# A gated mix of a Fourier layer and a token MLP on one core: operands of 512 columns in pairs of K tiles, PSUM banks in pairs

## The chip, the core and the metric

The kernel runs on one core of one Trainium2 chip. The metric is the device time of one execution in microseconds. Before the change its median over three runs is 1861.19 us (1860.97 to 1861.49).

A core has a matrix engine (TensorE, "PE" in the profile), whose weight loads are listed apart as "PEld", a vector engine (VectorE, "DVE"), a scalar engine (ScalarE, "ACT"), GpSimd ("POOL"), which here only issues DMAs, and SyncE ("SP"), which issues the loads. Each engine works through its own instructions in the order in which the program lists them and waits at an instruction until what it needs is there. SBUF is the on-chip memory that operands lie in, PSUM the one that matmuls write; PSUM has 8 banks of 512 float32 values per partition here.

## What is computed

```python
def _A_ref(x, dft_seq_re, dft_seq_im, dft_hid_re, dft_hid_im):
    a = jnp.einsum("bsd,ed->bse", x, dft_hid_re)
    b = jnp.einsum("bsd,ed->bse", x, dft_hid_im)
    return jnp.einsum("ts,bse->bte", dft_seq_re, a) - jnp.einsum("ts,bse->bte", dft_seq_im, b)

def _B_ref(x, w1, b1, w2, b2):
    h = _layernorm(x, axis=-1)
    u = _gelu(jnp.einsum("bsd,sf->bdf", h, w1) + b1)
    y = jnp.einsum("bdf,fs->bds", u, w2) + b2
    return y.transpose(0, 2, 1)

x = A_x
g = _sigmoid((x * gate_w).sum(-1, keepdims=True))
return g * _A_ref(x, ...) + (1 - g) * _B_ref(x, ...)
```

x is 2048 x 1024, the Fourier matrices are 2048 x 2048 and 1024 x 1024, w1 is 2048 x 3584 and w2 is 3584 x 2048, all float32.

## The kernel before

**Four stages.** Each large product is a stage, an object of a class derived from `Bilinear`: `Fourier` (q: x against the sequence matrices), `Mixed` (y: q against the hidden matrices), `Up` (u: w1 against the normalised x) and `Down` (o: w2 against u). They run one after another.

**26 products in place of 32.** A stage splits one operand into 4 x 4 blocks and the other into 4 x 2, and computes the 4 x 2 result with 26 block products instead of 32. The table `SCHEME` (line 48) lists for each product the signed sum of blocks of one operand, that of the other, and the signed result blocks to which it is added. The sums are formed on DVE (`add`, `sub`, lines 478 and 481), or by an accumulating DMA of POOL (`add_onto`, line 489); sums that return later are stored to DRAM (line 494). In the profile W names the operand that TensorE holds as weights, R the one that it streams.

**Three matmuls for one.** Each operand is split into a high half, rounded on ACT (line 508), and a low half, the difference, on DVE (lines 513 and 515). Lines 771 to 773 multiply high by high, high by low and low by high, each 128 x 128 weights against 128 x 512. A block holds `nk` K tiles of 128 rows: 4 in q, y and u, 7 in o. It gives `nm` x `nn` PSUM banks: 8 in q, 4 in y and o, 7 in u. `groups()` says in which steps the K tiles run; the last two always run together, bank by bank. One bank gets 3 matmuls a K tile. A product has 96 matmuls in q, 48 in y, 84 in u and o.

**Evictions and chains.** When a bank has its last K tile, each result block that reads it takes it over: first with a copy (`plain_copy`, on ACT or DVE), then with a multiply-add of one bank on DVE (`fused`, line 816). Where the signs of two products that follow each other agree well enough, the second goes on adding in the same banks (`self.chained`), and what it must not pass on is corrected by coefficients. PE then returns to a bank of which the eviction must be over. `self.reads` lists the blocks that read product j: one for most, two for some, three for one of u. In o every eviction is scaled by the gate, a scalar per partition (`hgate`, `ngate`).

**Order and memory.** Nothing of the order is written by hand. `Graph` collects tasks with a key (its due time in K steps) and `schedule()` plays them through with fixed costs; what is ready with the lowest key goes first. The order found is the program order of each engine. SBUF is two pools: 40 slots of 1024 columns ("f") and 23 of 512 ("h"); PSUM has 8 slots of one bank. Raw operands of 512 columns lie in h; the high and low halves of such an operand share one f slot in y and o (`pairs`) and lie in two h slots elsewhere. Result blocks lie in f slots, two banks to a slot.

In q only W has 512 columns, and R has 1024; in u only R has 512, and W has 896; in y and o both have 512.

Of the kernel before, what the change touches and what calls it, by code (L numbers as in the profile page):

```python
# [24 lines left out]
SLOTS = {"f": 40, "h": 23, "ps": 8}  # L25
# [3 lines left out]
HOP = 0.1  # L29
DMA_RATE = 330e3  # L30
# [240 lines left out]

class Task:
# [138 lines left out]
def gated_mix_kernel(  # L411
# [31 lines left out]
        "ps": (ctx.enter_context(tc.tile_pool(name="psum", bufs=8, space=bass.MemoryType.PSUM)), H),  # L443
# [138 lines left out]
    class Bilinear:  # L582
# [6 lines left out]
        pairs = False  # L589
        ahead = 3  # L590

        def __init__(self, name, nk, nm, nn, wn, rn, big, keep, order, extra, perm):
            self.name, self.nk, self.nm, self.nn = name, nk, nm, nn
            self.n = {"W": wn, "R": rn}
            self.big, self.perm = big, perm
            rows = [SCHEME[j] for j in order]

            self.small = "RW"[big == "R"]
            small = [r[1] for r in rows]
            self.again = {j: s for j in range(1, len(rows)) for s in (1, -1) if small[j] == [s * c for c in small[j - 1]]}  # L600
            self.kept = {}
            self.plan = {x: plan([None if x != big and j in self.again else r[x != big] for j, r in enumerate(rows)],
                                 extra[x != big], keep[x]) for x in "WR"}
            self.out = [r[2] for r in rows]
            self.val, self.saved, self.stored = {"W": {}, "R": {}}, {}, {}
            for x in "WR":
                for e in sorted(self.plan[x][1]):
                    for k in range(nk):
                        self.saved[x, e, k] = scratch(self.n[x], f"{name}_{x}{e}_{k}", 1)
            self.C, self.PS, self.half = {}, {}, {}  # L610
# [47 lines left out]
        def term(self, x, e, last, j, k, key):  # L658

            val, n = self.val[x], 16 if x == self.big else 8  # L660
            if (e, k) not in val:
                if e < n:
                    pi, pk, pj = self.perm
                    b = pi[e // 4] * 4 + pk[e % 4] if x == self.big else pk[e // 2] * 2 + pj[e % 2]
                    val[e, k] = self.block(x, b, j, k, key), 1
                else:
                    d, v = self.saved[x, e, k], slot(self.n[x], f"{self.name}_{x}{e}_p{j}_{k}")
                    load(key, v, d.t, (d,))
                    val[e, k] = v, self.stored[x, e, k]
            v, s = val.pop((e, k)) if last else val[e, k]  # L670
            return v, s, last and not (e < n and x in self.resident)

        def by_dma(self, x, j, k, o):
            return False

        def fresh(self, x, e, k, last):

            if (e, k) in self.val[x] or not last:
                return None
            if e < (16 if x == self.big else 8):  # L680
                pi, pk, pj = self.perm
                b = pi[e // 4] * 4 + pk[e % 4] if x == self.big else pk[e // 2] * 2 + pj[e % 2]
                return None if x in self.resident else (*self.source(x, b, k), 1)
            d = self.saved[x, e, k]
            return d.t, (d,), self.stored[x, e, k]

        def operand(self, x, j, k, key):
# [3 lines left out]
            for o, ((a, ca, la), (b, cb, lb)) in ops:  # L691
                if self.by_dma(x, j, k, o):
                    swap = self.fresh(x, a, k, la) is None
                    if swap:
                        (a, ca, la), (b, cb, lb) = (b, cb, lb), (a, ca, la)
                    src = self.fresh(x, a, k, la)
                    if src is not None and lb and fresh.get(b) != k and (b >= (16 if x == self.big else 8) or x not in self.resident):
                        held = (b, k) in self.val[x] or b < (16 if x == self.big else 8)
                        sb = self.val[x][b, k][1] if (b, k) in self.val[x] else self.stored.get((x, b, k), 1)
                        if held and ca * src[2] == cb * sb:  # L700
                            v, sb, _ = self.term(x, b, lb, j, k, key)
                            add_onto(key, v, *src[:2])
                            self.val[x][o, k] = v, cb * sb
                            if o in self.plan[x][1]:
                                d = self.saved[x, o, k]
                                self.stored[x, o, k] = cb * sb
                                fresh[o] = k
                                store(key + 1, d.t, d, v)
                            continue
                (va, sa, mine_a), (vb, sb, mine_b) = self.term(x, a, la, j, k, key), self.term(x, b, lb, j, k, key)  # L710

                mine_a, mine_b = mine_a and fresh.get(a) != k, mine_b and fresh.get(b) != k
                v = va if mine_a else vb if mine_b else slot(self.n[x], f"{self.name}_{x}s{o}_{k}")
                (add if ca * sa == cb * sb else sub)(key, v, va, vb)
                self.val[x][o, k] = v, ca * sa
                if o in self.plan[x][1]:
                    d = self.saved[x, o, k]
                    self.stored[x, o, k] = ca * sa
                    fresh[o] = k
                    store(key + 1, d.t, d, v)  # L720
            v, sv, _ = self.term(x, e, last, j, k, key)
            return v, s * sv

        def build(self):
            nonlocal step
            eps = 1
            for j in range(len(self.out)):
                self.during(j, step)
                for ks in self.groups():
                    ops = []  # L730
                    for k in ks:
                        pair, val = {}, {}
                        for x in "RW":
                            if x == self.small and j in self.again:
                                pair[x], s = self.kept[k]
                                val[x] = None, s * self.again[j]
                            else:
                                val[x] = self.operand(x, j, k, step)
                        s = val["R"][1] * val["W"][1]
                        if k == 0 and not self.chained[j]:  # L740
                            eps = s * self.sign[j]
                        flip = s != eps * self.sign[j]
                        for x in "RW":
                            if x not in pair:
                                v, s = val[x]
                                negate = flip and (x == "W" or self.small in pair)
                                pair[x] = self.split(x, step, v, j, k, negate)
                                if x == self.small:
                                    self.kept[k] = pair[x], -s if negate else s
                            elif x == self.small:  # L750
                                self.kept[k] = pair[x], val[x][1]
                        ops.append((pair["R"], pair["W"]))
# [3 lines left out]
        def split(self, x, key, v, j, k, negate):  # L756
            return split(key, v, f"{self.name}_p{j}_{x.lower()}_{k}", negate, self.pairs)

        def matmuls(self, j, ks, ops, eps):
            first, end = ks[0] == 0 and not self.chained[j], ks[-1] == self.nk - 1  # L760
            for m in range(self.nm):
                c = slice(m * P, (m + 1) * P)
                for n in range(self.nn):
                    if first:
                        self.PS[m, n] = View(Buf("ps", f"ps_{self.name}_p{j}_{m}_{n}"), 0, H)
                    bank, e = self.PS[m, n], slice(n * H, n * H + H)
# [425 lines left out]
```

## Time and profile before

| | us |
|---|---|
| median of the runs | 1861.19 |
| the profiled execution, its own time | 1859.57 |
| its span, first to last instruction | 1857.8 |
| TensorE busy (8122 matmuls) | 1848.7 |
| VectorE busy | 1687.8 |
| ScalarE busy | 893.7 |
| GpSimd busy | 249.7 |

The profile lists every instruction with its start and duration, which engine or DMA ended the idle time before it, and the DMA transfers. Its tables are read in four ways below: by stretches of time, with the busy time of each engine and (after "x") the instructions in the stretch; in order of time for one engine; by groups of like instructions; and along the chain of waits that ended last. The durations of matmuls overlap, since they are pipelined: the time that one costs is the distance of the starts. The same holds to a lesser degree for DVE and ACT.

### The profile page before, as it was taken

The page shows a single profiled execution, that of the slowest core. Times are in us where ns is not written, and L with a number is a line of the kernel's source. Part 1 is how long each engine was busy: PE and PEld are TensorE (multiplying, and loading weights), DVE is VectorE, ACT ScalarE, POOL GpSimd, SP SyncE. Part 2 cuts the span into 40 slices and gives each one's busy share as a digit, 9 for nine tenths or more (in the row PEclk, how much of TensorE's full clock was granted, in tenths as well). Part 3 has the DMA queues.
Part 4 walks back from the last instruction along what each step waited for, and adds up shares of the span by engine and source line. Part 5 has one row for each costly group of instructions (what it writes and reads, how often), then busy time and mean ns, then how long its engine had stood idle before and what let it go on. Part 6 is the DMA issues. An engine that isn't in the chain of part 4 may idle for free.

```text
span 1857.8 us, 24437 instructions
## 1 busy us (share of the span) xinstructions
PE 1848.7 (100%) x8122; PEld 1522.2 (82%) x8122; DVE 1687.8 (91%) x2443; ACT 893.7 (48%) x1379; POOL 249.7 (13%) x428
## 2 busy tenths in 40 slices
PE   9999999999999999999999999999999999999999
PEld 7888888888888888888888888888888888888787
DVE  8899679979979999999978699889799999998996
ACT  5443335644535555586554325345464535443442
POOL 1100010111022101112121211121120000001111
PEclk9999999999999999999999999999999999999999
DMA  9967478969698767989658798897988566675974
GB/s 381 332 229 257 166 241 317 332 250 392 225 317 306 215 229 241 329 287 342 223 191 293 254 356 318 285 369 252 357 310 285 164 204 205 213 230 120 273 199 99
DMA packets 199358, 491.88 MB, mean 265 GB/s; under 512 B 24832, under 2 KB 24832, under 8 KB 199232
## 3 DMA queue, kind: packets, MB, share of 16 engines
q1 hardware_dynamic: 159984, 369.72, 58.2%
q0 software_dynamic: 39104, 120.35, 19.7%
q8 instruction: 63, 1.03, 0.2%
q14 instruction: 63, 0.52, 0.1%
q10 hardware_dynamic: 144, 0.26, 0.0%
HBM read 375.41 MB, written 114.82 MB: 264 GB/s over the span
## 4 chain that ended last, share of the span: by engine, by line
PE 79%; DVE 11%; issue 5%; DMA 4%; POOL 1%; ACT 0%; SPq 0%; POOLq 0%; DVEq 0%; ACTq 0%
PE ps_q_p L773 10%; PE ps_q_p L772 10%; PE ps_q_p L771 10%; PE ps_u_p L773 9%; PE ps_u_p L772 9%; PE ps_u_p L771 9%; PE ps_o_p L771 5%; PE ps_o_p L772 5%; PE ps_o_p L773 5%; PE ps_y_p L771 3%; PE ps_y_p L773 3%; PE ps_y_p L772 3%; DVE o_W_p L478 1%; DVE y_c L816 1%; DVE o_p_r L515 1%
## 5 line engine op out<-in xcount | busy, mean ns | idle before, releaser
L771 PE MATMUL ps_q_p<-q_p_r_hi,q_p_w_hi 128*128 128x512 f32 x824 | 320.7, 389 | 1.1 <-ACT q_p_w_hi L508 1.1
L773 PE MATMUL ps_q_p<-q_p_r_hi,q_p_w_lo 128*128 128x512 f32 x824 | 320.6, 389 | 0.1
L772 PE MATMUL ps_q_p<-q_p_r_lo,q_p_w_hi 128*128 128x512 f32 x824 | 320.7, 389 | 0.0
L771 PE MATMUL ps_o_p<-o_p_r,o_p_w 128*128 128x512 f32 x728 | 284.5, 391 | 1.9 <-DVE o_c L816 1.6
L772 PE MATMUL ps_o_p<-o_p_r,o_p_w 128*128 128x512 f32 x728 | 283.3, 389 | 0.0
L773 PE MATMUL ps_o_p<-o_p_r,o_p_w 128*128 128x512 f32 x728 | 283.3, 389 | 0.0
L771 PE MATMUL ps_u_p<-u_p_r_hi,u_p_w_hi 128*128 128x512 f32 x728 | 283.2, 389 | 0.0
L773 PE MATMUL ps_u_p<-u_p_r_hi,u_p_w_lo 128*128 128x512 f32 x728 | 283.2, 389 | 0.0
L772 PE MATMUL ps_u_p<-u_p_r_lo,u_p_w_hi 128*128 128x512 f32 x728 | 283.2, 389 | 0.0
L771 PEld LDWEIGHTS ps_q_p<-q_p_r_hi,q_p_w_hi 128*128 128x128 f32 x824 | 154.7, 188 | 33.7 <-ACT q_p_w_hi L508 1.5
L773 PEld LDWEIGHTS ps_q_p<-q_p_r_hi,q_p_w_lo 128*128 128x128 f32 x824 | 154.7, 188 | 32.5 <-DVE q_p_w_lo L513 0.4
L772 PEld LDWEIGHTS ps_q_p<-q_p_r_lo,q_p_w_hi 128*128 128x128 f32 x824 | 154.7, 188 | 32.3 <-DVE q_p_r_lo L515 0.3
L508 ACT ACTIVATE o_p_r<-o_R_p 128x512 fp32r<-128x512 f32 x175 | 107.5, 626 | 134.2 <-DVE o_R_p L481 43.3
L508 ACT ACTIVATE q_p_r_hi<-q_R_p 128x1024 fp32r<-128x1024 f32 (+1 forms) x101 | 105.1, 1047 | 125.7 <-DVE q_R_p L478 70.3
L771 PEld LDWEIGHTS ps_o_p<-o_p_r,o_p_w 128*128 128x128 f32 x728 | 136.6, 188 | 34.5 <-DVE o_c L816 6.5
L508 ACT ACTIVATE o_p_w<-o_W_p 128x512 fp32r<-128x512 f32 x182 | 111.3, 626 | 110.1 <-DVE o_W_p L481 47.3
L508 ACT ACTIVATE u_p_w_hi<-u_W_p 128x896 fp32r<-128x896 f32 x104 | 97.8, 950 | 136.8 <-DVE u_W_p L478 91.2
L771 PE MATMUL ps_y_p<-y_p_r,y_p_w 128*128 128x512 f32 x416 | 162.5, 391 | 0.7 <-DVE y_c L816 0.5
L772 PE MATMUL ps_y_p<-y_p_r,y_p_w 128*128 128x512 f32 x416 | 161.9, 389 | 0.0
L773 PE MATMUL ps_y_p<-y_p_r,y_p_w 128*128 128x512 f32 x416 | 161.8, 389 | 0.0
L771 PEld LDWEIGHTS ps_u_p<-u_p_r_hi,u_p_w_hi 128*128 128x128 f32 x728 | 136.6, 188 | 28.6 <-DVE u_c L816 0.2
L773 PEld LDWEIGHTS ps_o_p<-o_p_r,o_p_w 128*128 128x128 f32 x728 | 136.6, 188 | 28.5
(150 smaller groups left out, 3283.4 us busy)
## 6 DMA issues: line engine op xcount, KB each, us to landing
q_R_p<-in_ct_dram SPq DMA_DIRECT2D x131, 512.0 KB, 6.9
u_W_p<-in_w_dram SPq DMA_DIRECT2D x136, 448.0 KB, 6.1
o_W_p<-in_w_dram SPq DMA_DIRECT2D x196, 256.0 KB, 5.2
o_R_p<-u SPq DMA_DIRECT2D x140, 256.0 KB, 4.6
u<-u_c POOLq DMA_DIRECT2D x126, 256.0 KB, 5.7
y_W_p<-q SPq DMA_DIRECT2D x99, 256.0 KB, 5.2
q<-q_c POOLq DMA_DIRECT2D x80, 256.0 KB, 6.0
q_W_p<-in_x_dram SPq DMA_DIRECT2D x75, 256.0 KB, 7.1
```

The costliest lines, as they stand in the source:

```text
L478: g.add({"DVE": dve(o.n)}, key, lambda e: nc.vector.tensor_add(o.ap, a.ap, b.ap), r=(a.reg, b.reg), w=(o.reg,))
L508: g.add({"ACT": act(v.n)}, key, lambda e: nc.scalar.activation(hi.ap, v.ap, AF.Copy, scale=-1.0 if negate else 1.0), r=(v.reg,), w=(hi.reg,))
L515: nc.vector.tensor_sub(lo.ap, v.ap, hi.ap.bitcast(F32))
L771: nc.tensor.matmul(bank.ap, wh.ap[:, c], rh.ap[:, e], start=a, stop=False, skip_group_check=True)
L772: nc.tensor.matmul(bank.ap, wh.ap[:, c], rl.ap[:, e], start=False, stop=False, skip_group_check=True)
L773: nc.tensor.matmul(bank.ap, wl.ap[:, c], rh.ap[:, e], start=False, stop=b, skip_group_check=True)
L816: lambda e: nc.vector.scalar_tensor_tensor(o.ap, ps.ap, scale, o.ap, op0=ALU.mult, op1=ALU.add),
```

## The change

An operand of 512 columns is handled for two K tiles at once. `unit` maps each K tile to its pair; `new` takes one f slot for both halves; raw blocks, sums, stored sums and the high and low halves are all of 1024 columns. Only the last K tile of o stays single. Operands of 1024 and 896 columns stay as they are.

PSUM has 4 slots of two banks. Two banks that follow each other are evicted by one instruction (`evacuate`), n before m; in u the seventh is alone. The key of an eviction is half a step lower (`EVAC`). In y and o the first two K tiles run together too (`groups`).

In o, blocks that end before the last product are accumulated without the gate and scaled by it in one ACT instruction a tile when they are done; the block that ends last is gated as before, bank by bank. The sums of w2 that an accumulating DMA made are all on DVE (`by_dma` no longer holds for any). Rows of h are normalised in halves. The pools are 49 f and 5 h slots. The start of the first product is written out as before, with W in two halves.

```diff
-SLOTS = {"f": 40, "h": 23, "ps": 8}
+SLOTS = {"f": 49, "h": 5, "ps": 4}
+EVAC = 0.5
...
+            self.unit = {x: [(k,) if n > H or nk - k == nk % 2 else (k - k % 2, k - k % 2 + 1) for k in range(nk)]
+                         for x, n in self.n.items()}
...
         def groups(self):
-            return [(k,) for k in range(self.nk - 2)] + [(self.nk - 2, self.nk - 1)]
+            return ([(0, 1)] if self.nm * self.nn == 4 else [(0,), (1,)]) + [(k,) for k in range(2, self.nk - 2)] + [(self.nk - 2, self.nk - 1)]
...
+        def new(self, x, name, u, parts=1):
+            n = self.n[x] * len(u)
+            return View(Buf("f" if n > H else "h", f"{self.name}_{x}{name}_{u[0]}", None, parts), 0, n)
+
-        def block(self, x, b, j, k, key):
-            src, r = self.source(x, b, k)
-            v = slot(self.n[x], f"{self.name}_{x}{b}_p{j}_{k}")
-            load(key, v, src, r)
+        def block(self, x, b, j, u, key):
+            v = self.new(x, f"{b}_p{j}", u, len(u))
+            for i, k in enumerate(u):
+                load(key, v.at(i, self.n[x]), *self.source(x, b, k))
             return v
...
+                if end and (i % 2 or i == count - 1):
+                    self.evacuate(j, i // 2, step + len(ks) + i / count - EVAC, i % 2 + 1, eps)
...
+        def new_bank(self, j, i):
+            b = self.PS[i - 1].buf if i % 2 else Buf("ps", f"ps_{self.name}_p{j}_{i}", None, 2)
+            self.PS[i] = View(b, i % 2 * H, H, i % 2)
+
+        def evacuate(self, j, i, key, count, eps):
+            bank = View(self.PS[2 * i].buf, 0, count * H, None if count == 2 else 0)
+            mn = [divmod(2 * i + t, self.nm)[::-1] for t in range(count)]
+            for q, coef in self.reads[j]:
+                b = self.perm[0][q // 2] * 2 + self.perm[2][q % 2]
+                o = self.C.get((b, i))
+                if o is None:
+                    o = self.C[b, i] = View(Buf("fh"[count == 1], f"{self.name}_c{b}_{i}", None, count), 0, count * H)
...
+                        self.copy(key, b, mn, o, bank, eps * coef)
+                else:
+                    self.accumulate(key, b, mn, o, bank, eps * coef)
+                if j in self.ends[b]:
+                    del self.C[b, i]
+                    for t, (m, n) in enumerate(mn):
+                        self.finish(key + 1, b, m, n, o.at(t, H), j)
...
     class Down(Bilinear):
...
-        def by_dma(self, x_, j, k, o):
-            return j > 1 and (k + j) % 7 in O_DMA
+        def by_dma(self, x_, j, u, o):
+            return j > 1 and (u[0] // 2 + j) % 4 in O_DMA
...
-        def accumulate(self, key, b, m, n, o, ps, coef):
-            i, t = (b // 2) * 4 + m, hgate if coef > 0 else ngate
-            fused(key, o, ps, t.t[:, i:i + 1], (t,))
+        def accumulate(self, key, b, mn, o, ps, coef):
+            if self.ends[b][0] < len(self.out) - 1:
+                return fused(key, o, ps, float(coef))
+            for t, (m, _) in enumerate(mn):
+                i, f = (b // 2) * 4 + m, hgate if coef > 0 else ngate
+                fused(key, o.at(t, H), ps.at(t, H), f.t[:, i:i + 1], (f,))
...
             if j == len(self.out) - 1:
                 store(key, dst, reg, o, "SP")
             else:
+                g.add({"ACT": act(H) + 0.15}, key, lambda e: nc.scalar.activation(
+                    o.ap, o.ap, AF.Copy, scale=hgate.t[:, i:i + 1]), r=(o.reg, hgate), w=(o.reg,))
                 g.add({"POOL": 0.9}, key, lambda e: nc.gpsimd.dma_start(dst, o.ap, accum_op=ALU.add),
                       r=(o.reg,), w=(reg,), nbytes=2.2 * P * o.n * 4)
```

More of the change, by code (lines that the diff above doesn't have):

```diff
@@ L731, in build @@
                     for k in ks:
-                        pair, val = {}, {}
                         for x in "RW":
[L734 to L739, printed above, removed]
+                            u = self.unit[x][k]
@@ L795, in c_slots @@
[L795 to L803 removed]
+            first, end, count = ks[0] == 0 and not self.chained[j], ks[-1] == self.nk - 1, self.nm * self.nn
```

275 lines of the change are left out of this document (123 added, 152 removed).

## The prediction

> **What bounds the kernel now.** I read the page's first lines first, then a table of stretches, one for each stage, with the busy time of every engine, then the list of who waited for whom on PE.
>
> ```profile
> span 1857.8 us, 24437 instructions
> PE 1848.7 (100%) x8122; PEld 1522.2 (82%) x8122; DVE 1687.8 (91%) x2443; ACT 893.7 (48%) x1379; POOL 249.7 (13%) x428
> ...
> core 0: us, PE busy (x) PEld busy (x) DVE busy (x) ACT busy (x) POOL busy (x), PEclk, DMA share, GB/s
> 5.55:573.50 567.95, 566.72 (x2496) 468.50 (x2497) 506.69 (x657) 267.60 (x401) 70.90 (x127) 1.00 0.81 289
> 573.50:858.70 285.20, 284.55 (x1250) 233.69 (x1249) 279.86 (x456) 169.07 (x271) 43.52 (x74) 1.00 0.81 267
> 858.70:1353.80 495.10, 495.10 (x2186) 409.84 (x2185) 432.61 (x573) 236.06 (x335) 87.14 (x163) 1.00 0.82 293
> 1353.80:1854.10 500.30, 498.36 (x2185) 408.86 (x2183) 467.03 (x758) 218.51 (x371) 47.91 (x63) 1.00 0.71 209
> 1854.10:1857.80 3.70, 0.00 (x0) 0.00 (x0) 0.75 (x1) 0.00 (x0) 0.00 (x0) 1.00 0.38 142
> ...
> PE ps_o_p L771 <- DVE o_c L816: 1.6, 5, 0.4
> PE pw L1128 <- DVE warm L1126: 1.2, 1, 1.2
> PE ps_q_p L771 <- ACT q_p_w_hi L508: 1.1, 1, 1.1
> PE ps_y_p L771 <- DVE y_c L816: 0.5, 2, 0.2
> ```
>
> The rows with times are stages q, y, u, o and the end. TensorE is full, at a granted clock of 1.00. In stage u nothing stops it: 26 products of 84 matmuls, 2184 in 495.10 us, are 226.7 ns a matmul. At that step q (2496 matmuls) needs 565.8 us, y (1248) 282.9 and o (2184) 495.1. What they took beyond is all that feeding PE better can give: q 2.1, y 2.3, o 5.2, in all 9.6 us. The change leaves count and shape of the matmuls as they are, so 1857.8 - 9.6 = 1848.2 us is the floor of the span, unless the first 5.55 us or the last 3.70 move. The question is what becomes of 9.6 us of stalls, and which are added.
>
> **The start of q.** The first products take the one large stall. The first three stretches are products 0, 1 and 2; then DVE and ACT in order of time, and the chain.
>
> ```profile
> 5.60:27.50 21.90, 21.90 (x97) 18.12 (x98) 18.79 (x23) 11.80 (x17) 3.96 (x7) 1.00 1.02 397
> 27.50:51.30 23.80, 22.57 (x98) 17.93 (x97) 22.40 (x27) 14.02 (x21) 2.70 (x5) 1.00 1.03 415
> 51.30:73.00 21.70, 21.70 (x97) 17.98 (x96) 17.84 (x21) 11.43 (x18) 0.54 (x2) 1.00 0.85 316
> ...
> 27.91 1.22 DVE L478 TENSOR_TENSOR q_R_p<-q_R_p,q_R_p 128x1024 f32<-128x1024 f32 x1
> 29.05 0.69 DVE L481 TENSOR_TENSOR q_W_p<-q_W_p,q_W_p 128x512 f32<-128x512 f32 x1
> 29.65 0.69 DVE L515 TENSOR_TENSOR q_p_w_lo<-q_W_p,q_p_w_hi 128x512 fp32r<-128x512 f32 x1
> 30.25 0.69 DVE L478 TENSOR_TENSOR q_W_p<-q_W_p,q_W_p 128x512 f32<-128x512 f32 x1
> ...
> 37.16 0.69 DVE L481 TENSOR_TENSOR q_W_p<-q_W_p,q_W_p 128x512 f32<-128x512 f32 x1 [0.63 <-DMA q_W_p<-in_x_dram]
> 40.64 0.68 DVE L513 SCALAR_TENSOR_TENSOR q_p_w_lo<-q_W_p,q_p_w_hi 128x512 fp32r<-128x512 f32 x1
> ...
> 22.48 14.59 DMA q_W_p<-in_x_dram
> ```
>
> Product 1 lasts 23.80 us, 2.0 longer than 96 x 0.2267 = 21.76: its last W block landed at 22.48 + 14.59 = 37.07, DVE could start on it at 37.16, and the last low half was done at about 41.3, while PE, 51 matmuls into the product, wanted its K tile at 27.50 + 51 x 0.2267 = 39.1. DMA is at 1.02 and 1.03 of its engines in both stretches, so what lands when is a matter of bytes in SP's order.
>
> **The change, part by part.**
>
> *DVE's price.* Its starts stand 1.14 us apart after a 1024-wide instruction (27.91 to 29.05) and 0.60 after a 512-wide one (29.05 to 29.65); the durations printed overlap by some 0.08. A pair made one saves 0.60 + 0.60 - 1.14 = 0.06 to 0.07 us. No row shows 1024 columns evicted from PSUM. I take 1.14, since the 512-wide evictions below go at the pace of the SBUF operations (0.60); the bounds are 1.0 and 1.2 (two singles). 258 such evictions at 0.06 more are 15 us of DVE over all stages, under 3 in y and in o (44 and 46 of them): nothing on PE's path while DVE has the room worked out next. Counted from the order in which both programs stand on DVE, its instructions fall from 2427 to 1529. Stage y goes from 471 of 512 columns (x 0.602 = 283.5 us) to 236 of 1024 (x 1.135 = 267.9); stage o from 781 (470 us) to 340 of 1024 and 114 of 512 (454.5 us; 14 sums of w2 that a DMA made are now DVE's). PE needs 282.9 and 495.1. So y, where DVE had no room at all, gets 15 us over its 285, and o 40 instead of 25.
>
> *Stalls of y and o: -1.6 and -4.2.* The stretches are product 19 of y and 14, 19, 20 of o; the DVE rows are the evictions at the turn to product 14.
>
> ```profile
> 781.30:793.30 12.00, 11.52 (x49) 8.78 (x49) 12.00 (x21) 7.07 (x11) 0.00 (x0) 1.00 1.03 384
> 1620.70:1640.70 20.00, 19.64 (x86) 15.63 (x85) 19.98 (x33) 9.08 (x17) 0.89 (x1) 1.00 0.78 248
> 1717.20:1738.00 20.80, 20.01 (x86) 15.55 (x86) 17.66 (x30) 8.33 (x15) 3.64 (x5) 1.00 0.97 257
> 1738.00:1758.30 20.30, 19.71 (x85) 15.51 (x84) 19.39 (x32) 6.89 (x12) 3.95 (x5) 1.00 1.06 306
> ...
> 779.42 0.68 DVE L816 SCALAR_TENSOR_TENSOR y_c<-ps_y_p,y_c 128x512 f32<-128x512 f32 x1
> 780.02 0.68 DVE L478 TENSOR_TENSOR y_W_p<-y_W_p,y_W_p 128x512 f32<-128x512 f32 x1
> ...
> 1620.11 0.74 DVE L816 SCALAR_TENSOR_TENSOR o_c<-ps_o_p,hgate,o_c 128x512 f32<-128x512 f32 x1
> 1620.76 0.74 DVE L816 SCALAR_TENSOR_TENSOR o_c<-ps_o_p,ngate,o_c 128x512 f32<-128x512 f32 x1
> ...
> 1622.74 0.74 DVE L816 SCALAR_TENSOR_TENSOR o_c<-ps_o_p,hgate,o_c 128x512 f32<-128x512 f32 x1
> ```
>
> Products need 10.9 and 19.04 us; these four lost 1.1, 1.0, 1.8 and 1.3. In the first and second DVE never rests (12.00 of 12.00, 19.98 of 20.00), and PE waits for a chained bank whose eviction stands behind operand work, or which two readers take eight evictions of 0.66 us to empty. Three things help: DVE's room; evictions asked for half a step earlier (`EVAC`); and in o no pointer scalar (0.66 from 1620.11 to 1620.76, against 0.60 in y), the gate being applied once a block. And grouping K tiles (0, 1) gives the last bank more time: a next product comes back to its last pair after two banks of six matmuls, 2 x 6 x 0.2267 = 2.72 us, where the last bank had three of three, 2.04. I take about 0.7 of y's 2.3 and 1.0 of o's 5.2 to be left, half of the two-reader turns staying as they are; the bounds are none and all.
>
> *The start: +2.6.* R loads and sums are as before, W's are for two K tiles at once. In SP's order the loads that product 1 needs now come before the R load of product 2, which takes the place in bytes (38 quarter-megabytes) of the W load that landed at 37.07. But DVE's order puts the sum that waits for this R load *ahead* of five operations that product 1 needs or that stand between: its second W pair's low half, R's sum for K tile 3, two low halves of product 2 (R and W), and R's low half. These are DVE's instructions 25 to 30 in the changed program:
>
> ```
> q_R8_p0_0 <- q_R8_p0_0, q_R11_p2_0     128x1024
> q_p1_w_2_lo <- q_W1_p0_2, q_p1_w_2_hi  128x1024
> q_R8_p0_3 <- q_R7_p1_3, q_R8_p0_3      128x1024
> q_p2_r_0_lo <- q_R8_p0_0, q_p2_r_0_hi  128x1024
> q_p2_w_2_lo <- q_W6_p1_2, q_p2_w_2_hi  128x1024
> q_p1_r_3_lo <- q_R8_p0_3, q_p1_r_3_hi  128x1024
> ```
>
> Six of 1.135 from 37.1 are 43.9, in place of 41.3. The bounds: the load comes early and the stall goes (-2.0); or 2.4 us later, the distance of the last loads (+5).
>
> *At nothing.*
>
> ```profile
> L1118 ACT ACTIVATE h<-h,rstd 128x1024 f32<-128x1024 f32 x16 | 18.3, 1142 | 0.1
> L1019 ACT ACTIVATE o_c<-ps_o_p,hgate 128x512 f32<-128x512 f32 x15 | 10.4, 690 | 7.8 <-PE ps_o_p L773 7.3 <-ACT o_p_r L508 0.2
> ...
> out_dram<-o_c POOLq DMA_DIRECT2D x28, 256.0 KB, 8.1
> ```
>
> ACT normalises h in 64 halves (x 0.69 = 44 us) instead of 32 rows (x 1.14 = 36.5), and scales 28 tiles of o (19 us): under PE in y, u and o, where ACT is busy 169 of 285, 236 of 495 and 219 of 500 us. The last 8 scalings come between the last eviction of two blocks and their accumulating DMAs. Product 25 hides them: it starts at 1854.1 - 19.04 = 1835.1, and 8 x 0.69 of ACT and 8.1 to landing end at about 1849. Without that cover some 5 us would show at the end. The gated evictions of the last product stay single, so the last 3.70 us stay. Fewer loads of double size carry the same bytes; the pools hold the same 206 KB a partition.
>
> *Sum.* 2.6 - 1.6 - 4.2 = -3.2 us. The profiled execution took 1859.57 us, 1.77 around its span of 1857.8; less 3.2 it is 1856.4. The median of the runs, 1861.19, lies 1.62 above it, so I forecast 1858.0.
>
> **The rivals.**
>
> *A, the stalls simply go.* With DVE ahead by 15 us in y and 40 in o and the start no worse than now, -2.3 - 5.2 with 0 to -2 at the start: 1851.6 to 1856. For it: DVE is full in the stretches with stalls. Against it: at 1717.20 DVE had pauses (17.66 of 20.80) and PE lost most, so there lateness was not lack of room.
>
> *B, a pair is too coarse.* In a chained product with two readers DVE needs 2 x 1.135 = 2.27 us for a pair of banks, of the 2.72 us before PE returns to it: 0.45 us to spare, less than the one 1.135 us operation that may be running on DVE. From the planner's sign table ten of the products of y and o are such. If each of their two pairs loses 0.7 us, that is 14 us, less what the freed DVE saves (about 5) and with the 2.6 of the start: 1873; with one pair in two late, 1866. It decides from nine late pairs of the twenty on. For it: before, the operations that could stand in the way were half as long. Against it: from the end of the first bank to the return to the last, the same turn had eight of 0.66 us to do in 6.13 before and has four of 1.135 in 5.44 now, 0.85 and 0.90 to spare. [...]
>
> *C, it does nothing for PE's waits.* What is late is late for DMA or slots, and only the start's price shows: 1861.2 to 1863.8. For it: the 0.97 and 1.06 of DMA in the last two products above.
>
> **How the numbers follow.** The forecast has 0.50, A 0.24, B 0.20, C 0.06. What a measurement of this kernel can tell from no change is 0.2%, 3.7 us: below 1857.5 is faster, above 1864.9 slower. My own case (1855 to 1862) lies across the first bound and gives 0.20 faster, 0.29 same, 0.01 slower; A is faster; B gives 0.18 slower, 0.02 same; C 0.04 same, 0.02 slower. That is 0.44, 0.35 and 0.21. The range goes from A's floor, 1851.6, into B at 1867: below nothing is to be had, above is half of B.
>
> **What would show it.** Product 1 of q: 26.4 us in place of 23.8, with DVE waiting for a q_R load just before the last sums (right), 21.8 (A). Stage y at about 283.6, o at about 496; B would show y or o longer than now, with PE's waits on the y_c and o_c evictions growing from 2.1 us in all. DVE's busy share should fall from 91% to about 88; u must stay at 495.1, and the step at 226.7 ns. A new wait of PE on a low half or a high half after product 1 would overturn the forecast: operands would come late, because raw pair, high and low halves of two K tiles now hold their slots together.

## The result and the profile after

The changed kernel takes 1881.7 us (median of four runs, 1877.99 to 1888.35) against 1861.3 beside it: a ratio of 1.0113, interval 1.0085 to 1.0142. The forecast was 1858.0. The profiled execution took 1888.35 us, the longest of the four; its page, its table of stretches (stages q, y, u, o and the end, columns as before) and its list of PE's waits:

```profile
span 1886.4 us, 22788 instructions
PE 1859.1 (99%) x8122; PEld 1529.8 (81%) x8122; DVE 1637.9 (87%) x1545; ACT 854.1 (45%) x1001; POOL 208.7 (11%) x365
...
5.60:583.60 578.00, 572.00 (x2496) 471.68 (x2497) 496.66 (x464) 255.96 (x310) 62.04 (x111) 0.99 0.79 287
583.60:877.60 294.00, 287.61 (x1249) 235.50 (x1248) 269.31 (x237) 156.66 (x177) 31.90 (x55) 0.99 0.77 255
877.60:1374.40 496.80, 495.64 (x2185) 409.85 (x2184) 422.12 (x402) 227.01 (x271) 83.25 (x155) 1.00 0.82 299
1374.40:1881.50 507.10, 499.69 (x2185) 411.40 (x2183) 447.65 (x442) 211.96 (x242) 31.33 (x41) 0.99 0.65 199
1881.50:1886.40 4.90, 0.00 (x0) 0.00 (x0) 1.41 (x2) 0.00 (x0) 0.00 (x0) 0.93 0.36 132
...
PE ps_y_p L774 <- DVE y_c L821: 5.5, 4, 3.5
PE ps_o_p L774 <- DVE o_c L821: 5.1, 4, 3.0
PE ps_q_p L774 <- ACT q_p_r_hi L515: 3.4, 2, 2.4
PE ps_q_p L775 <- DVE q_p_r_lo L522: 2.5, 2, 1.8
PE ps_o_p L774 <- ACT o_p_r_hi L515: 2.2, 1, 2.2
```

VectorE did what was expected of it: 4 points less busy, 898 instructions fewer. The time grew all the same: q by 10.1 us, y by 8.8, u by 1.7, o by 6.8, the end by 1.2, which is the 28.6 us between the spans. PE's waits on y_c and o_c evictions grew from 2.1 to 10.6 us, and it now waits for high and low halves in q and o. Summed over all distances of matmul starts above 0.2267 us, stalls grew from 9.1 to 26.7 us. Another 9.5 us were lost in stretches at a granted clock of 0.5 ("half clock" below), which the profile before does not show: 4.3 of them in q, 5.2 in y and o.

In y the turn from product 9 to 10 shows an eviction that comes too late. First VectorE, then PE, in order of time (start, duration, in brackets the idle time ahead and who ended it):

```profile
692.42 1.23 DVE L522 TENSOR_TENSOR y_p_w_lo<-y_W_p,y_p_w_hi 128x1024 fp32r<-128x1024 f32 x1
693.56 4.61 DVE L821 SCALAR_TENSOR_TENSOR y_c<-ps_y_p,y_c 128x1024 f32<-128x1024 f32 x4
698.09 1.22 DVE L485 TENSOR_TENSOR y_W_p<-y_W_p,y_W_p 128x1024 f32<-128x1024 f32 x1
...
695.01 0.39 PE L776 MATMUL ps_y_p<-y_p_r_hi,y_p_w_lo 128*128 128x512 f32 x1
696.06 0.47 PE L774 MATMUL ps_y_p<-y_p_r_hi,y_p_w_hi 128*128 128x512 f32 x1 [0.66 <-DVE y_c L821]
```

PE wanted the first pair back at 695.24, 0.23 us after the start at 695.01. That pair's last matmul had started at 692.3, ahead of the other pair's twelve; then VectorE worked at a low half until 693.56, and two readers took 2 x 1.13 us until 695.8. The four evictions together take from 693.56 to 698.09, 4.53 us: 1.13 us for 1024 columns of PSUM.

At 798 us more goes wrong at once:

```profile
793.29 1.23 DVE L485 TENSOR_TENSOR y_W_p<-y_W_p,y_W_p 128x1024 f32<-128x1024 f32 x1 [6.40 <-DMA y_W_p<-y_W]
794.43 1.22 DVE L522 TENSOR_TENSOR y_p_r_lo<-y_R_p,y_p_r_hi 128x1024 fp32r<-128x1024 f32 x1
795.64 1.22 DVE L520 SCALAR_TENSOR_TENSOR y_p_w_lo<-y_W_p,y_p_w_hi 128x1024 fp32r<-128x1024 f32 x1
796.78 1.22 DVE L821 SCALAR_TENSOR_TENSOR y_c<-ps_y_p,y_c 128x1024 f32<-128x1024 f32 x1
...
798.15 0.77 PE L774 MATMUL ps_y_p<-y_p_r_hi,y_p_w_hi 128*128 128x512 f32 x1 [3.50 <-DVE y_c L821]
798.71 0.63 PE L775 MATMUL ps_y_p<-y_p_r_lo,y_p_w_hi 128*128 128x512 f32 x1
799.14 0.63 PE L776 MATMUL ps_y_p<-y_p_r_hi,y_p_w_lo 128*128 128x512 f32 x1
```

VectorE stood 6.40 us at a sum that needed an accumulating DMA, the eviction PE wanted three places behind it; and from 796.86 the clock is at half: matmuls start 0.43 us apart instead of 0.23.

### The profile page after: what moved, and what is told of

The parts are those of the page before. It is cut to its first block, busy times and chain, and to the rows that moved or that the text cites. A ratio compares the mean times of both kernels' runs of the same rounds, so it can differ in the third digit from the quotient of the medians.

```text
span 1886.4 us, 22788 instructions
## 1 busy us (share of the span) xinstructions
PE 1859.1 (99%) x8122; PEld 1529.8 (81%) x8122; DVE 1637.9 (87%) x1545; ACT 854.1 (45%) x1001; POOL 208.7 (11%) x365
## 2 busy tenths in 40 slices
DMA packets 193873, 491.77 MB, mean 261 GB/s; under 512 B 23584, under 2 KB 23584, under 8 KB 193760
## 4 chain that ended last, share of the span: by engine, by line
PE 72%; DMA 10%; issue 9%; DVE 7%; POOL 1%; ACT 1%; SPq 0%; DVEq 0%; POOLq 0%; ACTq 0%
PE ps_q_p L775 9%; PE ps_q_p L776 9%; PE ps_q_p L774 9%; PE ps_o_p L774 7%; PE ps_o_p L775 7%; PE ps_o_p L776 7%; PE ps_y_p L774 4%; PE ps_u_p L774 4%; PE ps_u_p L775 4%; PE ps_u_p L776 4%; PE ps_y_p L775 4%; PE ps_y_p L776 4%; DMA o_W_p<-in_w_dram 2%; DMA q_R_p<-in_ct_dram 2%; DMA o_R_p<-u 1%
## 5 line engine op out<-in xcount | busy, mean ns | idle before, releaser
L774 PE MATMUL ps_o_p<-o_p_r_hi,o_p_w_hi 128*128 128x512 f32 x624 | 244.8, 392 | 7.4 <-DVE o_c L821 5.1
L775 PE MATMUL ps_o_p<-o_p_r_lo,o_p_w_hi 128*128 128x512 f32 x624 | 244.1, 391 | 0.0
L776 PE MATMUL ps_o_p<-o_p_r_hi,o_p_w_lo 128*128 128x512 f32 x624 | 244.0, 391 | 0.0
L774 PE MATMUL ps_y_p<-y_p_r_hi,y_p_w_hi 128*128 128x512 f32 x416 | 164.0, 394 | 6.4 <-DVE y_c L821 5.5
L776 PE MATMUL ps_y_p<-y_p_r_hi,y_p_w_lo 128*128 128x512 f32 x416 | 163.0, 392 | 0.0
L775 PE MATMUL ps_y_p<-y_p_r_lo,y_p_w_hi 128*128 128x512 f32 x416 | 163.0, 392 | 0.0
L775 PEld LDWEIGHTS ps_u_p<-u_p_r_lo,u_p_w_hi 128*128 128x128 f32 x728 | 136.7, 188 | 28.3
L776 PEld LDWEIGHTS ps_u_p<-u_p_r_hi,u_p_w_lo 128*128 128x128 f32 x728 | 136.7, 188 | 28.2
L774 PEld LDWEIGHTS ps_o_p<-o_p_r_hi,o_p_w_hi 128*128 128x128 f32 x624 | 117.8, 189 | 34.2 <-issue 5.8
L522 DVE TENSOR_TENSOR q_p_r_lo<-q_R_p,q_p_r_hi 128x1024 fp32r<-128x1024 f32 (+1 forms) x101 | 121.3, 1212 | 20.2 <-ACT q_p_r_hi L515 17.3
```

The lines of the kernel that those rows point to most:

```text
L522: nc.vector.tensor_sub(lo.ap, v.ap, hi.ap.bitcast(F32))
L774: nc.tensor.matmul(bank.ap, wh.ap[:, c], rh.ap[:, e], start=a, stop=False, skip_group_check=True)
L775: nc.tensor.matmul(bank.ap, wh.ap[:, c], rl.ap[:, e], start=False, stop=False, skip_group_check=True)
L776: nc.tensor.matmul(bank.ap, wl.ap[:, c], rh.ap[:, e], start=False, stop=b, skip_group_check=True)
```

## The experiments

My first theory, T, came from the stalls at 42, 308, 798 and 1511 us, where an operand is late or holds up the evictions behind it: the pairs of *operands* are at fault. Against it stood the prediction's rival B: the pairs of *banks* are too coarse. A third, E, blamed the earlier key of the evictions.

The table has the median of each run, its ratio to the kernel before, run beside it, the stages' times from first matmul to first matmul (o to the end of its last) and the lengths of products 1 and 13 of q (p1, p13). The last six columns are from the one profiled execution, which can lie some us from the median: 1888.35 beside 1881.7 for the changed kernel, 1867.1 beside 1862.5 for e7.

| | median us | ratio, interval | q | y | u | o | p1 | p13 |
|---|---|---|---|---|---|---|---|---|
| before | 1861.3 | | 568.0 | 285.2 | 495.1 | 500.3 | 23.8 | 21.8 |
| changed | 1881.7 | 1.0113 (1.0085-1.0142) | 578.0 | 294.0 | 496.8 | 507.1 | 26.7 | 28.6 |
| e1 | 1889.1 | 1.0160 (1.0138-1.0183) | 570.4 | 290.4 | 506.6 | 506.8 | 23.7 | 21.8 |
| e2 | 1866.0 | 1.0036 (1.0021-1.0050) | 575.7 | 284.1 | 495.0 | 499.7 | 25.5 | 27.9 |
| e3 | 1878.7 | 1.0098 (1.0082-1.0113) | 577.2 | 288.2 | 496.7 | 502.7 | 26.8 | 26.8 |
| e4 | 1881.1 | 1.0107 (1.0092-1.0123) | 576.8 | 291.4 | 496.5 | 502.9 | 27.0 | 26.5 |
| e5 | 1874.3 | 1.0080 (1.0062-1.0098) | 577.8 | 284.0 | 497.0 | 502.7 | 26.9 | 28.2 |
| e6 | 1869.9 | 1.0056 (1.0038-1.0074) | 579.6 | 282.9 | 496.3 | 498.6 | 24.3 | 21.8 |
| e7 | 1862.5 | 1.0010 (1.0000-1.0021) | 572.8 | 288.6 | 495.1 | 499.2 | 27.3 | 22.7 |
| e8 | 1861.6 | 1.0004 (0.9994-1.0013) | 569.0 | 286.4 | 495.1 | 499.4 | 24.0 | 22.5 |
| e9 | 1888.6 | 1.0152 (1.0138-1.0166) | 572.1 | 290.5 | 505.9 | 508.4 | 25.9 | 21.8 |
| e10 | 1864.2 | 1.0018 (1.0009-1.0027) | 571.3 | 282.8 | 496.9 | 503.1 | 26.3 | 22.5 |
| e11 | 1857.9 | 0.9984 (0.9975-0.9993) | 568.4 | 284.2 | 495.0 | 499.0 | 23.2 | 22.5 |
| e12 | 1853.3 | 0.9960 (0.9948-0.9973) | 569.8 | 282.9 | 495.1 | 496.9 | 24.5 | 22.5 |
| e13 | 1860.6 | 0.9998 (0.9989-1.0006) | 568.4 | 284.0 | 495.0 | 500.8 | 23.8 | 21.8 |
| e14 | 1860.4 | 0.9997 (0.9988-1.0006) | 569.7 | 282.9 | 495.1 | 501.8 | 25.6 | 21.8 |

**e1, operands single again, banks in pairs.** The core of the edit:

```diff
-SLOTS = {"f": 49, "h": 5, "ps": 4}
+SLOTS = {"f": 40, "h": 23, "ps": 4}
-            self.unit = {x: [(k,) if n > H or nk - k == nk % 2 else (k - k % 2, k - k % 2 + 1) for k in range(nk)]
+            self.unit = {x: [(k,) for k in range(nk)]
```

> Undone: operands go K tile by K tile again (one sum, one high and one low half each of 512 columns, pools of 40 and 23); kept: PSUM banks in pairs, evictions half a step earlier, first two K tiles grouped in y and o, gate of o at a block's end. Theory T (the loss comes from operands asked for two K tiles at once: DVE's queue stands at a sum whose load or accumulating DMA has not landed, evictions behind it, and PE stalls that pass some 2 us halve the clock): 1858 to 1865 us, no half-clock stretch, product 1 of q 22 to 24 us, product 13 of q 22, PE stalls on evictions under 3 us in all. Rival B (pairs of banks are too coarse): 1875 to 1885, stalls of PE on y_c and o_c evictions stay near 10 us. Rival E (earlier eviction keys): as B, with DVE waiting for PE some 80 us in all.

With the operands go three things that the kernel before has too: 14 sums of w2 by an accumulating DMA, h normalised by whole rows, and the first W without halves.

**e2, banks single again, operands in pairs.**

```diff
-SLOTS = {"f": 49, "h": 5, "ps": 4}
+SLOTS = {"f": 49, "h": 5, "ps": 8}
-                if end and (i % 2 or i == count - 1):
-                    self.evacuate(j, i // 2, step + len(ks) + i / count - EVAC, i % 2 + 1, eps)
+                if end:
+                    self.evacuate(j, i, step + len(ks) + i / count - EVAC, count, eps)
...
-            bank = View(self.PS[2 * i].buf, 0, count * H, None if count == 2 else 0)
+            bank = self.PS[i]
```

> Undone: each PSUM bank has a slot of its own and is evicted by itself with 512 columns; kept: operands in pairs of K tiles, the pools of 49 and 5, eviction keys, groups, gating at a block's end. Theory T (operand pairs): 1872 to 1888 us, product 1 of q still 26 to 27 us, and half-clock stretches of the same kind. Rival B (pairs of banks are too coarse): 1858 to 1866, PE's waits on y_c and o_c evictions back to some 2 us; q as in the changed kernel.

Theory T fell. e1, without the pairs of operands, is no faster than the changed kernel (1889.1): products 1 and 13 of q are back at 23.7 and 21.8 us, but y and o keep most of their loss, and u gets one of its own. e2, without the pairs of banks, gives back 15.7 of the 20 us. Both came out at or beyond the end that B expected (1875 to 1885, 1858 to 1866), and far from T. e2's stretches and PE's waits:

```profile
5.60:581.30 575.70, 569.90 (x2496) 470.69 (x2497) 504.00 (x559) 257.56 (x334) 63.12 (x112) 0.99 0.79 288
581.30:865.40 284.10, 283.22 (x1250) 234.19 (x1249) 268.71 (x277) 158.29 (x191) 31.18 (x53) 1.00 0.78 265
...
1360.40:1860.10 499.70, 496.56 (x2185) 409.33 (x2183) 449.73 (x489) 212.81 (x251) 31.22 (x41) 1.00 0.65 203
...
PE ps_o_p L774 <- DVE o_c L823: 3.1, 3, 1.8
...
PE ps_y_p L774 <- DVE y_c L823: 0.9, 1, 0.9
```

y and o are 1.1 and 0.6 us shorter than before the change; what e2 still loses, 7.7 us, lies in q. At the turn to y's product 10 VectorE does eight evictions where it did four:

```profile
682.95 1.22 DVE L522 TENSOR_TENSOR y_p_r_lo<-y_R_p,y_p_r_hi 128x1024 fp32r<-128x1024 f32 x1
684.09 2.48 DVE L485 TENSOR_TENSOR y_W_p<-y_W_p,y_W_p 128x1024 f32<-128x1024 f32 x2
686.49 5.12 DVE L823 SCALAR_TENSOR_TENSOR y_c<-ps_y_p,y_c 128x512 f32<-128x512 f32 x8
```

They take longer (5.12 us beside 4.61), but each is for one bank. The product starts at 690.1, and the first bank had its last matmul 18 ahead of that, at about 686: PE does not stop here.

**e3, the evictions' key half a step later again.**

```diff
-EVAC = 0.5
+EVAC = 0.0
```

> The one number EVAC goes from 0.5 to 0, so evictions get a key half a step later in the planner; all else as changed. Rival E (asked for early, evictions stand in DVE's queue ahead of operand work, and DVE waits for PE): DVE's waits for PE on u_c, o_c, q_c fall from 81 us to some 45, and the time to 1861 to 1868. Theory T: the time stays at 1875 to 1885, for the late sums and loads are not touched; product 1 of q 26 to 27 us.

VectorE's waits for PE at u_c, o_c and q_c evictions are 79.0 us, not 45; the interval overlaps the changed kernel's. Theory E fell: the key is not the cause.

**e4, no accumulating DMA in y.**

```diff
-Y_KEEP, Y_DMA, Y_GAP = 2, (1,), 99
+Y_KEEP, Y_DMA, Y_GAP = 2, (), 99
```

> The sums of y that an accumulating DMA of GpSimd made are DVE's instead; all else as changed. Theory T: the stall of 3.7 us at 798 us (DVE stands 6.4 us at a sum for that DMA, two evictions behind it) and the 6.8 us of half clock after it (3.4 us lost) go: product 18 of y 11 to 12 us in place of 14.6, 5 to 8 us less than the changed kernel in all, so 1872 to 1877. If the stall at 798 is the evictions' own (B): y stays at 293 us and the time within 2 us of the changed kernel's.

The half clock at 797 went and y is 2.6 us shorter, but at the same turn PE now waits 1.9 us for a high half, and 2.1 us for an eviction at 862. The time, 1881.1, is that of the changed kernel, not T's 1872 to 1877. The DMA made one stall large; it is not why there are stalls.

**e5, pairs of banks, but a longer way back to them.**

```diff
-            return ([(0, 1)] if self.nm * self.nn == 4 else [(0,), (1,)]) + [(k,) for k in range(2, self.nk - 2)] + [(self.nk - 2, self.nk - 1)]
+            if self.nm * self.nn == 4:
+                return [(0, 1, 2, 3)] if self.nk == 4 else [(0, 1, 2), (3, 4, 5, 6)]
+            return [(k,) for k in range(self.nk - 2)] + [(self.nk - 2, self.nk - 1)]
```

> All as changed, pairs of banks too, but more K tiles run together, bank by bank: in y all four, in o three and then four (in the changed kernel two and two, and two, single ones and two). PE now comes back to a pair after 24 matmuls in y (5.4 us) and after 18 or 24 in o (4.1 and 5.4) instead of 12 (2.7). Theory B (two evictions of 1.14 us, or one behind another instruction, do not fit into 2.7 us): PE's waits on y_c and o_c evictions fall from 10.6 us in all to under 3, y to 283 to 286 us and o to 496 to 500; q and u keep their losses, so 1862 to 1869 us. Theory T (late operands with evictions queued behind them): operands of four K tiles are wanted at once, PE waits more on high and low halves, y and o stay at 293 and 505 or grow: 1876 or more.

```profile
PE ps_o_p L776 <- DVE o_c L823: 4.7, 7, 1.5
...
PE ps_y_p L776 <- DVE y_c L823: 0.5, 1, 0.5
```

In y theory B is right: 284.0, and of 5.5 us of waits for y_c evictions 0.5 are left. In o half of it comes, 502.7 instead of 496 to 500, with 4.7 us of waits still, and so the time, 1874.3, misses B's 1862 to 1869. Six of o's seven late evictions are of the second pair, to which PE returns after 18 matmuls, not 24. Late operands, which T expected in y and o, cost 0.2 us there.

**e6, q's W operand single.** Beside single banks:

```diff
-SLOTS = {"f": 49, "h": 5, "ps": 8}
+SLOTS = {"f": 45, "h": 13, "ps": 8}
-            self.unit = {x: [(k,) if n > H or nk - k == nk % 2 else
+            self.unit = {x: [(k,) if n > H or name == "q" or nk - k == nk % 2 else
```

> Single banks as in e2, and in q alone the operand of 512 columns goes K tile by K tile again; pools 45 and 13 to house it. If the 7.8 us that q lost in e2 (products 1 and 13) come from W's pairs there: q back to 568 to 570 us, product 1 some 23.8 and product 13 21.8, and 1856 to 1860 us in all. If they come from the pools or from the earlier evictions: q stays at 574 to 577 and the time at 1864 to 1868.

Product 13 is back at 21.8 and product 1 at 24.3, as expected if W's pairs made them late. The time missed, 1869.9 for 1856 to 1860: product 4 now takes 31.8 us, PE waiting 6.6 us for a high half of R. With other pools the planner found another order, and I did not follow this further.

**e7, the row statistics earlier.** Single banks, and:

```diff
-STATS_AT, STATS_STEP = ("q", 12), 3
+STATS_AT, STATS_STEP = ("q", 7), 1.25
```

> Single banks and pairs of operands as in e2; the row statistics of x (16 loads of 512 KB, each with one pass of VectorE and three of ScalarE) are spread over products 7 to 11 of q, where the DMA engines are half idle, instead of 12 to 23. If product 13 of q is late because these loads stand in the DMA queue among the operands of a full stretch (DMA share 1.02 from 270 to 310 us): product 13 back to 21.8 us, 1858 to 1862 in all, product 1 still 25.5. If W's pairs alone crowd it: product 13 stays above 25, 1863 to 1868.

First e2, then e7, in the stretches from 280 to 310 us, product 13 starting at 292.3 and 294.5:

```profile
280.00:290.00 10.00, 10.00 (x46) 8.29 (x45) 9.83 (x12) 3.48 (x5) 1.07 (x2) 1.00 1.02 413
290.00:300.00 10.00, 10.00 (x45) 8.27 (x45) 10.00 (x12) 6.53 (x8) 0.53 (x1) 1.00 1.03 413
300.00:310.00 10.00, 5.99 (x23) 4.35 (x22) 9.82 (x11) 6.71 (x11) 1.06 (x2) 0.92 1.02 391
```

```profile
280.00:290.00 10.00, 10.00 (x46) 8.29 (x45) 9.67 (x11) 2.69 (x3) 1.08 (x2) 1.00 1.01 368
290.00:300.00 10.00, 10.00 (x46) 8.29 (x45) 10.00 (x12) 3.95 (x4) 1.06 (x2) 1.00 1.00 351
300.00:310.00 10.00, 9.32 (x42) 7.39 (x41) 10.00 (x11) 5.99 (x7) 1.06 (x2) 1.00 0.85 306
```

In e2 the DMA engines are full to the end of the stretch; q's loads issued from 279 to 288 us land after 9.4 to 11.5 us (medians of their kinds), and W's pairs, needed two K tiles at a time, stand among R's loads. In e7 the loads issued in that time land after 4.7 to 8.8 us, the DMA share falls after 300 (0.85), and product 13 loses 0.9 us instead of 6.1. Product 1, untouched by the edit, took 27.3 us in this execution, half clock among it.

But e7 moves the statistics' passes on VectorE and ScalarE along with their loads, and in e2 such passes stand right ahead of the halves of R for which PE waits, until 306.23 and 308.55 us:

```profile
303.87 1.04 ACT L1057 ACTIVATE x<-x 128x1024 f32<-128x1024 f32 x1
305.14 1.99 ACT L515 ACTIVATE q_p_r_hi<-q_R_p 128x1024 fp32r<-128x1024 f32 x2
...
306.13 1.22 DVE L1061 SCALAR_TENSOR_TENSOR xg<-x,gw 128x1024 bf16<-128x1024 f32 x1
307.28 2.35 DVE L522 TENSOR_TENSOR q_p_r_lo<-q_R_p,q_p_r_hi 128x1024 fp32r<-128x1024 f32 x2
```

VectorE has no pause there from 280.81 to 309.6 us. Whether the full DMA engines or the full order of the two engines counts for more was not tried.

**e8, the order at the start.** As e7, and:

```diff
+            if (x, j, u) == ("R", 2, (0,)):
+                lows = [t for t in g.tasks[:n] if "DVE" in t.engines and t.key == key - 2]
+                for t in g.tasks[n:]:
+                    if "DVE" in t.engines:
+                        t.deps.update(lows)
```

> As e7, and on VectorE the first sum of q's product 2, which waits for the last load of the start, stands behind the low halves of product 1 instead of ahead of two of them. By the prediction's step for the start: product 1 falls from 25.5 to 22 to 24 us, no half-clock stretch at 42 us, and 1855 to 1859 in all. If the loads themselves set product 1: it stays at 25 to 26, and the time is that of e7.

Product 1 is 24.0 us and has no half clock. The time did not follow: 1861.6 is not to be told from e7. y takes 3.5 us more than the 282.9 of its matmuls; the largest stall, 1.9 us, is at 783 us, where VectorE is idle 7.24 us ahead of a W sum.

**e9, e1 with another pool for u's last bank.**

```diff
-                    o = self.C[b, i] = View(Buf("fh"[count == 1], f"{self.name}_c{b}_{i}", None, count), 0, count * H)
+                    o = self.C[b, i] = View(Buf("f", f"{self.name}_c{b}_{i}", None, count), 0, count * H)
```

> As e1 (single operands, pairs of banks), but the result tile of u's seventh bank lies in a slot of the large pool, as before the change, not in one of the 23 small ones, of which ScalarE waited 8.8 us for one in e1. If e1's extra 10 us in u (506.6 against 496.8 us) are that shortage: u 495 to 499 and 1876 to 1882 in all, y and o as in e1 (290 and 507), for PE's return to a pair after 2.7 us is the same with single operands (theory B). If pairs of banks cost u more beside single operands: u stays at 505 or more and the time at 1885 or more.

The second case came, 1888.6, and the expectation has an error: before the change that tile lay in the small pool too. u stays at 505.9, now with PE waiting 5.6 us for high halves of W. y and o are slow as in e1, with single operands: that part is B's. Why u loses 11 us when pairs of banks meet single operands stays open; what else e1 and e9 put back is not excluded either.

**e10 to e12, the repairs together.** e10 has the edits of e4, e5, e7 and e8 on the changed kernel; e11 those of e4, e7 and e8 on e2; e12 adds e5's to e11.

> Pairs of banks and of operands as changed, with the four repairs at once: K tiles grouped as in e5, the order at the start as in e8, row statistics as in e7, no accumulating DMA in y as in e4. By the sum of what each gave: q 570, y 284, u 497, o 502 and 9 around them: 1862 to 1865 us; what is over 1857 then is what pairs of banks cost in u and o. If the repairs hinder each other: 1868 or more.

> Single banks, pairs of operands, the start of e8, the statistics of e7 and no accumulating DMA in y. If the 2 us stall at 783 us in e8 is again VectorE standing at a sum for that DMA with an eviction behind it: y 283 to 284 us in place of 286.4, and 1856.5 to 1860 us. If it is the evictions' own: as e8, 1860 to 1863.

> As e11 with the K tiles of y and o grouped as in e5, so that PE returns to a bank later still. If what o loses in e8 (499.5 of 495.1 us) is late evictions: o 496 to 498 and 1854 to 1858 us, faster than before the change. If operands wanted earlier take it back: o at 500 or more, PE waiting on high and low halves, 1859 or more.

All three came out within 1 us of the first case of their expectations. With pairs of banks the repairs give 1864.2; the same with single banks (e12) 1853.3, 0.4% below the kernel before and the fastest here. e10 and e12 differ in the banks alone, so that even with all repairs the pairs of banks cost 10.9 us. e12's y and u and o:

```profile
575.10:858.00 282.90, 282.90 (x1249) 234.23 (x1248) 267.27 (x275) 160.08 (x192) 25.31 (x47) 1.00 0.76 264
858.00:1353.10 495.10, 495.10 (x2186) 409.93 (x2185) 430.30 (x481) 231.41 (x292) 83.00 (x154) 1.00 0.83 300
1353.10:1850.00 496.90, 496.06 (x2185) 409.47 (x2183) 449.30 (x486) 212.18 (x254) 30.97 (x41) 1.00 0.67 204
```

**e13 and e14, the wider grouping on the kernel before.** e13 is the kernel before with e5's `groups` alone, e14 adds e4's edit.

> The kernel before, with the K tiles of y and o grouped as in e5 and e12, and nothing else: operands and banks single. If the gain of e12 (7.4 us below before) is the wider grouping alone: y 283 to 284, o 496 to 498, q 568, 1853 to 1857 us. If VectorE, busy 279.9 of 285.2 us in y, has no room without the pairs of operands: y stays at 285, o at 498 to 500, 1859 to 1863 us; then the pairs of operands are worth some 3 to 6 us.

> As e13, and the sums of y that the accumulating DMA made are VectorE's, as in e12. Operands and banks single. If VectorE's room decides: the 512-wide sums it takes over more (0.60 us each) do not fit into y, y 287 us or more and the time over that of e13. If its room does not matter: y 283 to 284, and 1853 to 1857.

e13's y:

```profile
573.80:857.80 284.00, 283.53 (x1250) 234.12 (x1250) 281.70 (x461) 169.47 (x273) 44.27 (x75) 1.00 0.80 265
```

VectorE is busy 281.70 of 284.00 us, and there is no wait for an eviction; the 1 us left is a late high half in product 3. In e14, with more sums on VectorE, y is at its floor of 282.9. Room was not what y lacked. But neither run is faster than the kernel before (1860.6 and 1860.4 us); both miss the 1853 to 1857 that they would take if the grouping alone made e12's gain. In o nothing is lost but in product 21, 5.6 and 6.6 us, where a high half of W is late; e12 has no such stall there. Whether its pairs of operands are what spares it, or its later gating or its sums of w2, was not tried.

## Why the prediction was wrong

**VectorE's price and room: right.** 1.14 us was forecast for an eviction of two banks, 1.13 measured; a busy share of 88% was forecast, 87 measured.

**What the room would buy: the step that failed.** "Stalls of y and o: -1.6 and -4.2" took late evictions for a lack of room on VectorE, with help from earlier keys and a longer way back to the last bank. e13 shows y without them on a VectorE just as full, by giving PE a longer way back. What decided was the time from a bank's last matmul to PE's return to it. Before, that was 18, 15, 12 and 9 matmuls for the four banks of a product of y or o (4.1 to 2.0 us), and the stalls over 0.4 us in y and o lay at the third and fourth. Now it is 12, 2.7 us, for either pair: longer for the last bank, as forecast, but shorter for the first, while one eviction takes 1.13 us in place of 0.60. Nine turns of y and o are now late by 0.4 us or more on an eviction, eight of them at the first pair. The prediction's own case counted the turn from the first bank or pair to the last ("0.85 and 0.90 to spare"); that the tightest point had moved to the first pair stood in rival B alone. In place of -5.8 us, y and o gained +15.6, of which 5.2 are half clock. u, which was to stay, gained 1.7, with 1.3 us of waits for evictions, and the end 1.2: the gated evictions "stay single", but both now wait for the pair's last matmul.

**Rival B: the right mechanism, in number partly by luck.** Its 2.72 us and its 0.45 to spare are what the first pair has, and its 14 us lie near the 13.0 that PE lost at the nine late turns and the 15.7 that e2 gives back. But its sum is not theirs. Its ten turns after two readers are eight by the kernel's sign table (four in y, four in o), and only five of the nine late turns, 6.4 us, are among them: those into products 10 and 23 of y and 7, 14 and 19 of o. Into y's product 19 it was a sum that waited for a DMA, into 7 an operation that waited for ACT, into 5 a copy on ACT behind three high halves: whatever stands in an engine's order ahead of the eviction decides, not a second reader alone. The rival deserved more than its 0.20. e2, which breaks the evictions up again, has VectorE busy 89% of the span, 1653.4 us, 15.5 more than the changed kernel, and the time is 15.7 us shorter.

**The start, +2.6: right in mechanism, in size by luck.** VectorE waited for the R load and then ran the six operations in the order forecast, from 35.60 to 42.5 us where 37.1 to 43.9 was forecast, for the load came 1.5 us earlier. Product 1 took 26.7 for 26.4 forecast, but 1.5 of it is half clock; the stalls alone are 3.4 us, 1.4 more than before. With the order repaired product 1 is 24.0, 23.2 and 24.5 in e8, e11 and e12, though 26.3 in e10, 1.5 of it half clock.

**Product 13 of q, 6.8 us: not in the forecast.** "Fewer loads of double size carry the same bytes" was costed at nothing because the bytes are the same (491.88 MB before, 491.77 after). Of the 6.8 us, 2.8 are half clock and 4.0 are stalls. With W single again they are gone (e6), and with the statistics moved away nearly (e7), so both have a part; by which way they meet, in the DMA queue or in the order of VectorE and ScalarE, stays open. The prediction's own sign for this, a new wait on a high or low half after product 1, appeared at 308 us.

**The step of 226.7 ns: right as a pace, wrong as a rule.** The floor was built on a clock of 1.00 throughout; in the profiled execution of the changed kernel the clock is at 0.50 for 23.9 us, at four of the stalls, and the matmuls there take 9.5 us more.

## What to carry to other kernels

Before making evictions larger, compute the time from a PSUM bank's last matmul to TensorE's return to it, and compare it with the eviction plus whatever may stand ahead of it in that engine's order: at the turn to y's product 10 it was 2.7 us against 2 x 1.13, with a low half of 1.14 ahead. The busy share did not tell this here. Making the return longer, here by running more K tiles bank by bank, removed y's stalls on evictions while VectorE stayed 99% busy in that stage (e13). It did not shorten the kernel before as a whole: in o another stall came, 3.1 us at a late high half. And when two K tiles' operands are fetched together, look at the stretches where the DMA engines and VectorE have no pause: here product 13 of q came late in such a stretch with pairs (27.9 us in e2, DMA share 1.02, VectorE busy 9.82 of 10.00 us), and not with single K tiles (21.8 us in e1 and e6).

## What the hardware showed unasked

In the profiled execution of the changed kernel the stretches at a clock of 0.50 within the four stages start at 42.51, 308.75, 796.86 and 1510.25 us; the first lasts 3.41 us, the others 6.83. The last three start 266.24, 754.35 and 1467.73 us after the first, which is 78, 221 and 430 times 3.413 us, half the longer length: in this execution they lie on one grid. Two pairs of steps of 3.4 us from e1, the second pair 374 times 3.413 us after the first:

```profile
425.20:428.60 3.40, 1.66 (x8) 1.05 (x7) 3.40 (x5) 0.00 (x0) 1.07 (x3) 1.00 0.84 269
428.60:432.00 3.40, 3.40 (x17) 2.80 (x16) 3.40 (x5) 2.31 (x3) 0.46 (x1) 1.00 0.90 273
1701.80:1705.20 3.40, 1.57 (x8) 1.01 (x7) 3.40 (x6) 0.93 (x2) 0.87 (x1) 1.00 0.00 0
1705.20:1708.60 3.40, 3.40 (x10) 2.62 (x9) 3.40 (x6) 3.36 (x7) 2.34 (x4) 0.50 0.76 101
```

PE is busy 1.66 us in the first and 1.57 in the third, 8 matmuls each. After the third the clock is 0.50 and 10 matmuls are counted, after the first it stays at 1.00 with 17; seven matmuls are 7 x 0.2267 = 1.6 us. In the changed kernel the steps right ahead of the four stretches have PE busy for 0.66, 1.02, 1.20 and 1.45 us, and the longest distance of matmul starts that reaches into each is 2.0, 2.6, 3.7 and 3.1 us above the 0.2267. A fifth of 2.3 us, at 1707 us, has no half clock behind it: it lies across two steps of the grid, with PE busy 2.39 and 2.27 us in them. So e1's expectation, by which stalls past some 2 us halve the clock, fits four of these five. Nor does a border show in PE's busy time: with 1.70 us (e10 at 39.6 us) the clock is 0.50 in the next step, with 1.66 (e1 at 425) and 1.78 (e3 at 1637) it is 1.00.

The four runs of the changed kernel have mean clocks of 0.993 (1888.4 us) to 0.998 (1878.0), and spread over 10 us. As an estimate, at the 9.5 us that the profiled execution lost for its 0.007, those 0.005 are some 7 of the 10 us.
